# A one-core layer of recurrent attention and feed-forward: small matmuls placed between two weight chunks, a shorter GpSimd program, and one load cut in four

## The chip, the core and the metric

The kernel runs on one core of one Trainium2 chip. The metric is the device time of one execution in microseconds (us). Three runs of the kernel before gave 1005.17, 1005.47 and 1006.03 us; the median is 1005.47. Engines are named as in the profile: PE (TensorE) with PEld (its weight loads), DVE (VectorE), ACT (ScalarE), POOL (GpSimd), SP (the engine that only issues transfers here).

## The reference, cut to what matters

```python
def _A_ref(x, mem0, Wq, Wk, Wv, Wo, seg_len):      # 32 heads of 128, seg_len 32, 8 memory rows
    mem = mem0
    for s in range(n_seg):                          # 64 segments, one after another
        h = jnp.concatenate([mem, x[:, 32*s:32*s+32]], axis=1)      # 40 rows
        q, k, v = (einsum('btd,dhe->bhte', h, W) for W in (Wq, Wk, Wv))
        p = softmax(where(mask, q @ k^T * scale, -1e9))
        o = einsum('bhte,hed->btd', p @ v, Wo)
        mem = o[:, :8]                              # the next segment starts from it
        outs.append(o[:, 8:])
h  = x + _A_ref(layernorm(x), mem0, Wq, Wk, Wv, Wo, 32)
h2 = h + relu_glu(layernorm(h), W_gate, W_up, W_down)               # 640 -> 1728 -> 640
```

x has 2048 rows of 640 numbers, bf16. The 64 segments form one chain, since the 8 memory rows of one segment are inputs of the next.

## The kernel before

The whole program is written out by hand, with no loop left on the chip: `add` appends an operation to the list of one engine, `solve` finds which earlier operations it has to wait for, and each engine then runs its list in order. What follows on a list never passes what stands before it.

The kernel has three parts.

1. The opening. SP issues the three attention weights in chunks of 1 MB (five for each of K, Q and V, the chunks cutting the 640 rows into 128s), then eight pieces of the output weight Wo, then rows of x. `project` multiplies a set of 32 rows by one chunk for all heads; the K and Q products of three row sets follow the chunks as they land. `first_values` does the value products: chunks 0 to 2 in L770, chunks 3 and 4 in L896, behind the scores of segment 0 (`scores`, L894 and L895). Then come the softmax of segment 0, the products with the values (`pv_mem`), and the output product for the memory rows: `wo_pairs` in four groups (L920) into bank T0, and `wo_pass` for the other half of the heads into bank P3. Between these stand calls of `keep_busy`, whose products nobody reads: they are written to bank T1 over and over. With cut 2 each of its 512-column products is issued as two of 256 columns, with cut 4 as four of 128. `fold_split(T0, ...)` and `to_act_split(1, P3)` turn the result into the 8 memory rows of segment 1.

2. The segments 1 to 63, L945 on. Each segment projects its rows by K, Q and V, takes scores and softmax, and multiplies by Wo. The end of a segment is the narrow place: `wo_split` and `wo_pass` on PE; then DVE transposes a bank into TA (L602), ACT moves a part of it into SA (L604), SA is summed up (L606, on POOL in most segments and on DVE where s % 4 is 1), DVE transposes the other bank into TBf (L614) and adds SA to it (L615, the tile act_r). The next segment's first projection reads act_r. POOL's list in a segment is short: a wait, the copy `late_q` into Qo (L483), in some segments the copy `late_o` into oTe (L563), a wait, and the sum L606. In segment 60 (NSEG - 4) POOL also copies rows of act_r into act_e (L1087); segment 61 projects them.

3. The feed-forward, from segment 62 on mixed with the last segments. Its first block of 512 normalised rows was put aside in xn2_d and is loaded into xn2T by one transfer in segment 62 (L996); the gate and up weights are loaded in pieces from L1031 on. `gate_up` waits for all four keys of xn2T.

Before all this POOL writes the masks: `mca` by affine_selects (L298 and L302), then `mbd`.

The parts that the change and the prediction touch stand below.

Of the kernel before, what the change touches and what calls it, by code (L numbers as in the profile page):

```python
# [9 lines left out]
ALU = mybir.AluOpType  # L10
# [16 lines left out]
class _Graph:  # L27
# [10 lines left out]
    def add(self, eng, fn, r=(), w=(), dma=False):  # L38
        if eng == "pool" and not dma:
            r, w = tuple(r) + (("pool",),), tuple(w) + (("pool",),)  # L40
        op = _Op(eng, fn, tuple(r), tuple(w), dma)
        self.ops.append(op)
        return op
# [120 lines left out]
def build_kernel(nc, A_x, A_mem0, A_Wq, A_Wk, A_Wv, A_Wo, A_seg_len, B_W_gate, B_W_up, B_W_down, out):  # L164
# [3 lines left out]
    SEG = int(A_seg_len)  # L168
    F = B_W_gate.shape[1]
    assert (S, D, M, H, Dh, SEG, F) == (2048, 640, 8, 32, 128, 32, 1728)  # L170
    NSEG = S // SEG
    DC = D // 128
# [12 lines left out]
    xn2_d = nc.dram_tensor("xn2_d", [128, DC, TB], BF16)  # L185
# [9 lines left out]
    W = ar.alloc("W", [128, 3, DC, HD], BF16)  # L195
# [6 lines left out]
    xn2T = [ffn.alloc("xn2T0", [128, DC, TB], BF16)]  # L202
# [18 lines left out]
    mca = ar.alloc("mca", [128, 4, 2, SEG], BF16)  # L221
# [34 lines left out]
    def bank(b):  # L256
        return ps[:, b * 512:(b + 1) * 512]
# [5 lines left out]
    T0, T1 = 2, 3  # L263
    P0, P1, P2, P3 = 4, 5, 6, 7
# [8 lines left out]
    add = G.add  # L273

    def B(n):
        return ("B", n)
# [7 lines left out]
    for i in range(2):  # L284
        add("dve", lambda v, i=i: v.memset(oT[i][:], 0.0), w=[("oT", i, n, kh) for n in "mx" for kh in range(2)])
        add("pool", lambda p, i=i: p.memset(act_r[i][:], 0.0),
            w=[("act", i, j, "m") for j in range(4)] + [("act", i, "x")] + [("act", i, "x", j) for j in range(4)])
# [6 lines left out]
    for g in range(4):  # L294
        for j in range(4):
            for r in range(2):
                sl, n = mca[32 * g:32 * g + 32, j, r, :], 0 if r == g % 2 else 1 + j
                add("pool", lambda p, sl=sl, n=n: p.affine_select(sl, sl, [[1, SEG]], ALU.is_ge, 0.0,  # L298
                                                                  base=M if n == 0 else M * (n - 1) - RID,
                                                                  channel_multiplier=-1), r=[("mca",)], w=[("mca",)])  # L300
                if n > 1:
                    add("pool", lambda p, sl=sl, n=n: p.affine_select(sl, sl, [[0, SEG]], ALU.is_ge, 0.0,  # L302
                                                                      base=-M * (n - 1), channel_multiplier=1),
                        r=[("mca",)], w=[("mca",)])
    add("pool", lambda p: p.memset(mbd[:], 0.0), w=[("mbd",)])
    for g in range(4):
        for lo, hi, c in ((0, 1, g), (1, 5, g ^ 1)):
            add("pool", lambda p, g=g, lo=lo, hi=hi, c=c: p.memset(mbd[32 * g:32 * g + 32, lo:hi, 8 * c:8 * c + 8], BIG),
                r=[("mbd",)], w=[("mbd",)])
        for n in range(1, 5):  # L310
            sl = mbd[32 * g:32 * g + 32, n, :]
# [11 lines left out]
    def dma(dst, src, r=(), w=(), eng="sp"):  # L323
        add(eng, lambda e: e.dma_start(dst, src), r=r, w=w, dma=True)  # L324
# [121 lines left out]
    def place(s):  # L446
        return (s - 2) // 4 % 2, (s - 2) % 4
# [17 lines left out]
    def scores(s, hf, ks=range(4)):  # L465

        p, _ = place(s)

        def f(pe):
            for k in [4 * hf + n for n in ks]:  # L470
                for a in range(2):
                    for g in range(4):
                        h = head(k, g)
                        o, q = 160 * (g % 2) + 40 * (k % 4), 32 * (g ^ a)
                        i = pe.matmul(bank((P0, P1)[hf])[q:q + 32, o:o + 40],  # L475
                                      (Ko if a == 0 else Ke[p])[:, h, :], Qo[:, h, :], start=True, stop=True,
                                      skip_group_check=True)
            return i
        add("pe", f, r=[("Ko", hf), ("Qo", hf), ("Qo", "e"), ("Ke", p, hf)], w=[B((P0, P1)[hf])])
# [120 lines left out]
    def fold_split(bk, eng):  # L600

        add("dve", lambda v: v.transpose(TA[:].rearrange("p b c j -> p (b c j)"), bank(bk)[:, 0:320]), r=[B(bk)], w=[("TA",)])  # L602
        for lo, to in SWAP:
            add("act", lambda a, lo=lo, to=to: a.activation(SA[to:to + 64], TA[lo:lo + 64, 1, :, 0:M], ACTF.Copy),  # L604
                r=[("TA",)], w=[("SA", to)])
        add(eng, lambda v: v.tensor_tensor(SA[:], SA[:], TA[:, 0, :, 0:M], ALU.add), r=[("TA",), ("SA", 0), ("SA", 64)],  # L606
            w=[("SA", 0), ("SA", 64)])
        for lo, to in SWAP:
            add("act", lambda a, lo=lo, to=to: a.activation(fold[to:to + 64].rearrange(flat), bank(bk)[lo:lo + 64, 160:320],
                                                            ACTF.Copy), r=[B(bk)], w=[("fold",)])  # L610
# [138 lines left out]
    xe, xke = act_e[0], [("acte", 0)]  # L749
# [16 lines left out]
    def first_values(chunks):  # L766
        for c in chunks:
            for (a, ks), bks in zip((PASSES[0], PASSES[2]), OB[2]):
                project(a, ks, 2, (0, 1), bks, (c,))
# [109 lines left out]
        add("dve", lambda v: v.tensor_tensor(hT[par][:, j, :], g1[gi][:, :], bank(bu), ALU.mult),  # L879
            r=[B(bu), ("g1", gi)], w=[("hT", par, j)])  # L880

    def keep_busy(n, cut=1):
        wide = 512 // cut

        def f(pe):
            for g in range(4 * n):
                o = 32 * (g % 4)
                for q in range(cut):
                    i = pe.matmul(bank(T1)[o:o + 32, 0:wide], xe[:, 0, :], W[:, 2, 0, 0:wide], start=True, stop=True,  # L889
                                  skip_group_check=True)  # L890
            return i
        add("pe", f, r=xke + [("W", 2, 0)], w=[B(T1)])

    scores(0, 0)  # L894
    scores(0, 1)  # L895
    first_values(range(3, DC))  # L896
    for hf in range(2):
        exp_mem(0, hf)
        mask_mem(0, hf)
# [19 lines left out]
    for g in range(4):  # L919
        wo_pairs(0, T0, g)  # L920
        if g:
            keep_busy(4, (1, 2, 2, 4)[g])
    fold_split(T0, "pool")
    for g in range(3):
        wo_pass(0, P3, (1,), (g,))
# [19 lines left out]
    for s in range(1, NSEG):  # L945
# [16 lines left out]
        if s > 0:  # L962
            a, ks = pass_act(s)
            held, parts = fill_of(s)
            for i in range(2):
                project(a, ks, 1, (i,), ((P2, P3)[i],), *WAYS[i], held=i == 1 and held[0], parts=parts[i])
                to_tok((P2, P3)[i], i, "act")
                if last and i == 1:
                    load_piece(("Ko", 0), "act")
                flip(i, Ko, i, [("Ko", i)])  # L970
            if s % 4 == 2 and more:
                row_std(n_rows(nb + 1))
                row_scale(xl, ("xl",), n_rows(nb + 1), xl, ("xl",), "pool")
            if s % 4 == 1 and e2 is not None:
                row_std(128)
                row_scale(xt, ("xt",), 128, xt, ("xt",), "pool")
            pv_x(s - 1, 0)
            norm_x(0)
            if s % 4 == 0 and e2 is not None:
                add_attn(xt[:, :], xt, at, [("xt",), ("at",), ("rx",)], [("xt",)], "pool")  # L980
                dma(h_d[128 * e2:128 * e2 + 128, :], xt[:, :], r=[("xt",)], w=[("h_d", e2)])
            if s % 4 == 2:
                merge_v(s, 1)
            if not last:
                for i in range(2):
                    project(a, ks, 0, (i,), ((P0, P1)[i],), *WAYS[i], held=i == 1 and held[1], parts=parts[2 + i])
                    to_tok((P0, P1)[i], 2 + i, "act")
                    flip(2 + i, Qo, i, [("Qo", i)])
                    if i == 0:
                        norm_x_late(0)  # L990
                        flip_ox(s - 1, (0,))
            else:
                norm_x_late(0)
                flip_ox(s - 1, (0,))
            if s == NSEG - 2:
                dma(xn2T[0][:, :, :], xn2_d[:, :, :], r=[("xn2_d", u) for u in range(4)] + [("Wdone", 0)],  # L996
                    w=[("xn2", 0, u) for u in range(4)])
            project(a, ks, 2, (0,), (P2,), range(4), held=not last and held[2])
            scores(s, 0, (0, 1))
            project(a, ks, 2, (0,), (P2,), (4,))  # L1000
            scores(s, 0, (2, 3))
            if not last:
                exp_mem(s, 0)
                mask_mem(s, 0)
            to_v(P2, Vp, 0, ("Vp",), "act")
            if last:
                load_piece(("Vp", 0), "act")
            if s % 4 == 1 and ln:
                flip_rows(chunks_of(at[:, :]), xl, ("xl",), ("at",))
                if more:  # L1010
                    ln1_load(nb + 1, xl, ("xl",))
# [39 lines left out]
        if s == NSEG - 2:  # L1051
            p = 1 - place(s + 1)[0]
            add("pool", lambda o, p=p: o.tensor_copy(Qo[:, :, M:32], Qe[p][:, :, M:32]), r=[("Qe", p, i) for i in range(2)],
                w=[("Qo", i) for i in range(2)])
# [8 lines left out]
            dma(xt[:, :], x_ap[128 * e2:128 * e2 + 128, :], w=[("xt",)])  # L1063
            load_attn(at, e2, [], ("at",))
        wo_split(par, P1)
        fold_split(P1, "dve" if s % 4 == 1 else "pool")
        wo_pass(par, P3, (1,))
        to_act_split(s + 1, P3)
        if s >= 1:
# [15 lines left out]
        if s == NSEG - 4:  # L1085
            p, j = place(NSEG - 1)
            add("pool", lambda o, p=p, j=j: o.tensor_copy(act_e[1 - p][:, :, M:32], act_r[p][:, j, :, M:32]),  # L1087
                r=[("act", p, "x", j), ("act", p, "x")], w=[("acte", 1 - p)])


    def down_part(par, u, bks, js, hfs=(0, 1)):
# [71 lines left out]
    s = NSEG - 1  # L1163
# [37 lines left out]
    for b in range(NBLK):  # L1201
# [4 lines left out]
        for j in range(FC):  # L1206
# [8 lines left out]
            if b == 0 and j == 5:  # L1215
                for q, src in enumerate((B_W_gate, B_W_up)):
                    for e in range(2):
                        r0 = FR * (q ^ e)
                        dma(Wt[:, e, :, r0:r0 + FR], src[:, FM:F].rearrange("(c p) f -> p c f", p=128),
                            r=[("Wdone", 0), ("hT", 0, 5)], w=[("Wt", q, e)])  # L1220
# [74 lines left out]
```

## Time and profile before

One execution was profiled: 1004.47 us in all, of which the span from the first to the last instruction is 1002.7 us.

| what | value |
|---|---|
| span of the profiled execution | 1002.7 us |
| its time in all | 1004.47 us |
| runs shown (3) | 1005.17 to 1006.03 us, median 1005.47 |
| busy: DVE, ACT, POOL | 715.6, 524.9, 167.8 us |
| opening, up to the first K product of segment 1 | 0 to 58.33 us |
| attention segments, up to the first gate product | to 813.44 us |
| feed-forward | to the end |
| one segment, from its first product with values (L663) to the next | 12.03 to 12.33 us; 13.1 us for the one that ends at segment 63 |
| PE instructions: matmuls and weight loads | 26097 and 24920 |

A row of the timeline gives start, duration, engine, line, operation, tiles, shape and count; in brackets at its end stand the engine's idle time before it and what ended that. In the chain of waits each piece has a start, a duration and a name; "issue" means that nothing the profile shows was waited for. The row of a stretch gives its bounds, its length, the busy time of each engine with its count of instructions, the granted TensorE clock, the share of the DMA engines' time, and GB/s.

### The profile page before, as it was taken

The page shows a single profiled execution, that of the slowest core. Times are in us where ns is not written, and L with a number is a line of the kernel's source. Part 1 is how long each engine was busy: PE and PEld are TensorE (multiplying, and loading weights), DVE is VectorE, ACT ScalarE, POOL GpSimd, SP SyncE. Part 2 cuts the span into 40 slices and gives each one's busy share as a digit, 9 for nine tenths or more (in the row PEclk, how much of TensorE's full clock was granted, in tenths as well). Part 3 has the DMA queues.
Part 4 walks back from the last instruction along what each step waited for, and adds up shares of the span by engine and source line. Part 5 has one row for each costly group of instructions (what it writes and reads, how often), then busy time and mean ns, then how long its engine had stood idle before and what let it go on. Part 6 is the DMA issues. An engine that isn't in the chain of part 4 may idle for free.

```text
span 1002.7 us, 56369 instructions
## 1 busy us (share of the span) xinstructions
PE 970.9 (97%) x26097; PEld 537.8 (54%) x24920; DVE 715.6 (71%) x1863; ACT 524.9 (52%) x1330; POOL 167.8 (17%) x416
## 2 busy tenths in 40 slices
PE   3789999999999999999999999999999999999998
PEld 1255555556555555555556555655555554344443
DVE  2558787878888887888788878787878756345332
ACT  0456666666666666666666666566666643122121
POOL 7011202021302130222022212111110010000000
PEclk9899999999999999999999999999999999999999
DMA  9921212121222122111312131211121168413100
GB/s 374 417 96 36 53 29 53 28 56 55 54 41 54 48 54 46 48 54 47 53 41 63 48 55 40 41 41 39 40 40 34 44 175 242 103 20 93 27 14 26
DMA packets 73103, 73.34 MB, mean 73 GB/s; under 512 B 42304, under 2 KB 59680, under 8 KB 70944
## 3 DMA queue, kind: packets, MB, share of 16 engines
q1 hardware_dynamic: 70736, 68.44, 24.5%
q8 instruction: 200, 3.28, 1.4%
q10 hardware_dynamic: 2128, 1.31, 0.5%
q14 instruction: 39, 0.32, 0.1%
HBM read 37.04 MB, written 6.55 MB: 43 GB/s over the span
## 4 chain that ended last, share of the span: by engine, by line
PE 93%; DMA 3%; SPq 2%; DVE 1%; issue 1%; ACT 0%; POOL 0%; DVEq 0%; ACTq 0%
PE ps L386 47%; PE ps L850 10%; PE ps L359 7%; PE ps L574 7%; PE ps L591 7%; PE ps L634 4%; PE ps L1100 3%; DMA W<-in_A_Wv_dram 3%; PE ps L475 2%; PE ps L663 2%; PE ps L528 2%; SPq L324 1%; DMA Wd<-in_B_W_down_dram 0%; PE ps L889 0%; PE ps L863 0%
## 5 line engine op out<-in xcount | busy, mean ns | idle before, releaser
L386 PE MATMUL ps<-W,act_r 128*32 128x512 bf16 (+1 forms) x8369 | 454.4, 358 | 2.9 <-DVE act_r L615 1.8
L386 PEld LDWEIGHTS ps<-W,act_r 128*32 128x32 bf16 x8369 | 212.9, 96 | 168.3 <-DVE act_r L615 33.1
L410 ACT ACTIVATE tok<-ps 128x512 bf16<-128x512 f32 x190 | 109.4, 594 | 57.1 <-PE ps L386 48.7
L386 PE MATMUL ps<-W,act_e 128*32 128x512 bf16 x1224 | 120.8, 385 | 8.2 <-DMA W<-in_A_Wv_dram 4.2
L405 DVE STREAM_TRANSPOSE Ko<-tox 128x512 bf16<-128x512 bf16 x128 | 89.8, 702 | 38.9 <-ACT tox L410 36.6
L483 POOL COPY Qo<-Qe 128x256 bf16<-128x256 bf16 x64 | 28.0, 437 | 529.4 <-DVE oT L548 522.4
L410 ACT ACTIVATE tox<-ps 128x512 bf16<-128x512 f32 x134 | 79.6, 598 | 53.1 <-PE ps L386 32.0
L554 DVE STREAM_TRANSPOSE oT<-tox 128x512 bf16<-128x512 bf16 x128 | 94.2, 736 | 0.0
L405 DVE STREAM_TRANSPOSE Qo<-tok 128x512 bf16<-128x512 bf16 x124 | 85.5, 690 | 0.8
L359 PE MATMUL ps<-W,act_e 128*32 128x512 bf16 x856 | 85.5, 387 | 0.0
L574 PE MATMUL ps<-Wo,oT 128*32 128x160 bf16 x4032 | 82.4, 233 | 0.9 <-issue 0.9
L591 PE MATMUL ps<-Wo,oT 128*32 128x320 bf16 x2016 | 80.4, 300 | 0.0
L574 PEld LDWEIGHTS ps<-Wo,oT 128*32 128x32 bf16 x4032 | 71.4, 97 | 9.7 <-DVE oT L548 3.1
L410 ACT ACTIVATE Vp<-ps 128x512 bf16<-128x512 f32 x127 | 75.2, 592 | 0.7 <-ACT Vp L410 0.5
L878 ACT ACTIVATE g<-ps 128x512 bf16<-128x512 f32 x52 | 30.1, 593 | 80.1 <-PE ps L850 80.1
L604 ACT ACTIVATE SA<-TA 64x40 f32<-64x40 f32 x126 | 29.5, 234 | 75.8 <-DVE TA L602 75.0
L879 DVE TENSOR_TENSOR hT<-g,ps 128x512 bf16<-128x512 bf16 x52 | 35.7, 687 | 40.7 <-PE ps L850 38.7
L491 ACT ACTIVATE Pm<-ps 128x64 bf16<-128x64 f32 x126 | 28.2, 224 | 69.8 <-PE ps L475 69.7
L850 PE MATMUL ps<-xn2T,Wu 128*128 128x512 bf16 x259 | 64.5, 379 | 0.1
L850 PE MATMUL ps<-xn2T,Wg 128*128 128x512 bf16 x247 | 61.8, 379 | 1.3 <-issue 1.0
L591 PEld LDWEIGHTS ps<-Wo,oT 128*32 128x32 bf16 x2016 | 53.1, 97 | 15.3 <-DVE rm L538 0.9
L548 DVE STREAM_TRANSPOSE oT<-om 128x128 bf16<-128x128 bf16 x126 | 39.1, 310 | 31.1 <-ACT om L540 31.1
(113 smaller groups left out, 1441.0 us busy)
## 6 DMA issues: line engine op xcount, KB each, us to landing
VM<-Vp SPq DMA_DIRECT2D x126, 65.0 KB
VM<-Vp SPq DMA_DIRECT2D x63, 130.0 KB
W<-in_A_Wk_dram SPq DMA_DIRECT2D x5, 1024.0 KB
W<-in_A_Wq_dram SPq DMA_DIRECT2D x5, 1024.0 KB
W<-in_A_Wv_dram SPq DMA_DIRECT2D x5, 1024.0 KB
Wo<-in_A_Wo_dram SPq DMA_DIRECT2D x8, 640.0 KB
attn_d<-wtok SPq DMA_DIRECT2D x248, 7.5 KB
xt<-in_A_x_dram SPq DMA_DIRECT2D x16, 160.0 KB
```

The costliest lines, as they stand in the source:

```text
L359: return pe.add_instruction(mybir.InstMatmult(name=nc.get_next_instruction_name(), engine=mybir.EngineType.PE, ins=[pe.lower_ap(rhs), pe.l ...
L386: ins = pe.matmul(*b, start=(c == ends[0]), stop=(c == ends[1]), skip_group_check=True)
L405: add("dve", lambda v: v.transpose(dst[:, 16 * i:16 * i + 16, 0:32], tok[t][:, :].rearrange("p (h f) -> p h f", f=32)), r=tok_keys(t), w=keys)
L410: add("act", lambda a: a.activation(dst, src, ACTF.Copy), r=r, w=w)
L548: add("dve", lambda v: v.transpose(ap(oT[par], 160 * hf, [[40, 4], [320, 4], [1, 8]]), ap(om, 128 * hf, [[1, 4], [4, 32]])), r=[("om", hf) ...
L554: add("dve", lambda v, kh=kh: v.transpose(ap(oT[p], 160 * kh + M, [[320, 4], [40, 4], [1, 32]]), ap(tox, 128 * kh, [[256, 4], [1, 4], [4, ...
L574: i = pe.matmul(bank(bk)[32 * gg:32 * gg + 32, 0:160], src[:, hb, 0:32], w[:, gg], start=(hb == CH[16 * halves[0]]), stop=(hb == CH[-1]), ...
L591: i = pe.matmul(bank(bk)[32 * q:32 * q + 32, 0:320], src[:, hb, 0:32], w, start=(n == 0), stop=(n == 7), skip_group_check=True)
L634: ins = pe.matmul(bank(bk)[32 * q:32 * q + 32, 0:320], src[:, hb, 0:32], w[:, 2 * (q % 2):2 * (q % 2) + 2], start=(i == 0), stop=(i == 15) ...
L850: ins = pe.matmul(bank(bk), w[:, c, lo:lo + 128], xn2T[par][:, c, :], start=(c == 0), stop=(c == DC - 1))
L878: add("act", lambda a: a.activation(g1[gi][:, :], bank(bg), ACTF.Relu), r=[B(bg)], w=[("g1", gi)])
L879: add("dve", lambda v: v.tensor_tensor(hT[par][:, j, :], g1[gi][:, :], bank(bu), ALU.mult), r=[B(bu), ("g1", gi)], w=[("hT", par, j)])
```

## The change

Five edits:

- `keep_busy` loses its cut and gets a number of columns. The calls between the groups of `wo_pairs` issue 16 products of 512 columns each (before: 32 of 256, 32 of 256, 64 of 128). A new call of 80 products of 32 columns stands between value chunk 3 and value chunk 4. PE's list has as many instructions as before.
- In `mca`, four affine_selects of 32 columns become one over 4 x 32. POOL's list is three instructions shorter from there on.
- The load of xn2T in segment 62 becomes four transfers: chunks 0, 1, 2, and 3 with 4.
- L606 of segment 61 goes from DVE to POOL.
- The copy L1087 also waits for segment 61's memory rows in act_r (L615).

```diff
+                pat = [[1, SEG]]
+                if g == 0 and n == 0:
+                    if j:
+                        continue
+                    sl, pat = mca[0:32, :, r, :], [[0, 4], [1, SEG]]
-                add("pool", lambda p, sl=sl, n=n: p.affine_select(sl, sl, [[1, SEG]], ALU.is_ge, 0.0,
+                add("pool", lambda p, sl=sl, n=n, pat=pat: p.affine_select(sl, sl, pat, ALU.is_ge, 0.0,
...
-    def keep_busy(n, cut=1):
-        wide = 512 // cut
+    def keep_busy(n, cols=512):
...
             for g in range(4 * n):
                 o = 32 * (g % 4)
-                for q in range(cut):
-                    i = pe.matmul(bank(T1)[o:o + 32, 0:wide], xe[:, 0, :], W[:, 2, 0, 0:wide], start=True, stop=True,
-                                  skip_group_check=True)
+                i = pe.matmul(bank(T1)[o:o + 32, 0:cols], xe[:, 0, :], W[:, 2, 0, 0:cols], start=True, stop=True,
+                              skip_group_check=True)
...
-    first_values(range(3, DC))
+    first_values((3,))
+    keep_busy(20, 32)
+    first_values((4,))
...
         wo_pairs(0, T0, g)
         if g:
-            keep_busy(4, (1, 2, 2, 4)[g])
+            keep_busy(4)
...
             if s == NSEG - 2:
-                dma(xn2T[0][:, :, :], xn2_d[:, :, :], r=[("xn2_d", u) for u in range(4)] + [("Wdone", 0)],
-                    w=[("xn2", 0, u) for u in range(4)])
+                for n, (lo, hi) in enumerate(((0, 1), (1, 2), (2, 3), (3, DC))):
+                    dma(xn2T[0][:, lo:hi, :], xn2_d[:, lo:hi, :], r=[("xn2_d", u) for u in range(4)] + [("Wdone", 0)],
+                        w=[("xn2", 0, n)])
...
-        fold_split(P1, "dve" if s % 4 == 1 else "pool")
+        fold_split(P1, "dve" if s % 4 == 1 and s != NSEG - 3 else "pool")
...
-                r=[("act", p, "x", j), ("act", p, "x")], w=[("acte", 1 - p)])
+                r=[("act", p, "x", j), ("act", p, "x"), ("act", *place(s + 1), "m")], w=[("acte", 1 - p)])
```

## The prediction, made before the changed kernel ran

> **What bounds the kernel.** I began with the page's busy times, its chain and its queues:
>
> ```profile
> PE 970.9 (97%) x26097; PEld 537.8 (54%) x24920; DVE 715.6 (71%) x1863; ACT 524.9 (52%) x1330; POOL 167.8 (17%) x416
> ...
> q8 instruction: 200, 3.28, 1.4%
> ...
> PE 93%; DMA 3%; SPq 2%; DVE 1%; issue 1%; ACT 0%; POOL 0%; DVEq 0%; ACTq 0%
> ```
>
> PE sets the time, so what counts is where PE stands still or runs at a lower clock. The second row is the program itself: 3.28 MB in 200 packets is 16 KB each, and 26097 + 24920 = 51017 PE instructions over 200 packets are 255 each, so q8 brings PE's code in pages of about 256 instructions. Next the chain of waits, in the opening and around segment 62:
>
> ```profile
> 14.26 28.38 DMA W<-in_A_Wv_dram
> 42.64 0.04 issue
> ...
> 51.98 1.50 issue
> ...
> 805.21 0.92 issue
> ```
>
> The opening waits for value chunk 4 until 42.64. The two long "issue" pieces are stops of PE in the middle of a row of like products, with no semaphore to wait for. Beside them I put the trace's records of q8's packets and PE's list counted out (a product with its own weight load is two). Counted so, the stops lie a whole number of 256s apart (186 of them); they are page borders, those of pages 4 and 190. A packet starts at 51.02 and takes 1.10, and PE resumes at 53.47; another starts at 803.76, takes 0.89, and PE resumes at 806.13. So a page can be used about 1.35 to 1.5 us after its packet ends. A page's packet follows the moment at which PE enters the page before it: usually 0.4 to 1.4 us later, but 3.5 us later (37.96 to 41.49, 47.49 to 51.02) while the weights stream, and 2.0 us (801.77 to 803.76) behind the xn2T load.
>
> Third, POOL around three ends of segments:
>
> ```profile
> 178.45 0.27 POOL L606 TENSOR_TENSOR SA<-SA,TA 128x40 f32<-128x40 f32 x1 [0.47 <-ACT SA L604]
> ...
> 190.78 0.27 POOL L606 TENSOR_TENSOR SA<-SA,TA 128x40 f32<-128x40 f32 x1 [0.76 <-DVE TBf L614]
> ...
> 202.82 0.27 POOL L606 TENSOR_TENSOR SA<-SA,TA 128x40 f32<-128x40 f32 x1 [0.46 <-ACT SA L604]
> ```
>
> The middle one comes 0.29 us late (idle 0.76 against 0.47), with its input ready; it is on the chain (190.79, 0.27, POOL SA L606), and the segment takes 12.33 instead of 12.04. The same is seen at 384.02 and 577.18, each 128 POOL instructions later, which is the size of an 8 KB page of the other engines (q14).
>
> Fourth, the clock and PE's work in stretches of 3.41 us:
>
> ```profile
> 35.53:38.95 3.42, 1.98 (x82) 0.71 (x62) 0.86 (x2) 0.00 (x0) 0.00 (x0) 1.00 1.01 422
> 38.95:42.36 3.41, 1.36 (x52) 0.41 (x33) 0.63 (x4) 1.00 (x4) 0.00 (x0) 1.00 1.00 410
> 42.36:45.77 3.41, 2.30 (x33) 0.71 (x28) 1.71 (x3) 1.20 (x2) 0.00 (x0) 0.50 1.02 411
> 45.77:49.19 3.42, 3.42 (x54) 1.70 (x41) 2.82 (x9) 2.37 (x3) 0.44 (x1) 0.50 1.02 416
> 49.19:52.60 3.41, 2.79 (x111) 2.52 (x104) 0.58 (x2) 2.79 (x6) 0.02 (x1) 1.00 1.01 409
> ```
>
> After a stretch with 1.36 us of PE work the granted clock is 0.50 for two stretches; after one filled with work it is 1.00 again.
>
> **The change, part by part.**
>
> *POOL's three instructions.* The three affine_selects themselves (0.20 to 0.27 each) end long before the masks are read and are worth nothing. But the page borders now fall three instructions later in the list: not at L606 but at the next segment's late_q copy (L483). That copy is read some 7 us later; 0.29 of delay to it, and to the late_o copy behind it, still lets L606 start in time (the copy at 189.63 would end at 190.32, and SA comes at 190.35). Gain 3 x 0.29 = 0.86. Bounds: 0 if the cost moves with L606, 0.9.
>
> *Segment 60's copy and segment 61's sum.* L615 at 782.44 takes 0.29 beside the copy L1087 at 782.40; at 794.66, with no copy beside it, 0.20. With the added wait the copy follows L615: 0.09. Behind the copy on POOL stand late_q and nothing due before 791; act_e is read by segment 61's fillers from 790 on. The sum on POOL is 0.27 against 0.20 on DVE, but no longer delays L614 there (794.16, 0.20, then 794.28); the fillers end at about the same time. Between 0 and 0.1; I take 0.05. Together 0.14, so that these and POOL make **1.0**.
>
> *Four transfers.* SP issues 4 instead of 1; the one took 0.58, neighbours 0.42 and 0.59, so 1.0 to 1.8 more. SP idles from 800.63 to 801.50 and from 801.92 to 803.27 (2.2 us), which hides it; the piece of Wg behind it slips by up to 1 us and is first read at 813.44. With that cover gone, the VM transfers at 803.27 would be late for 810.3. What it buys: in the records, xn2T's 128 packets of 5120 B run from 801.2 to 803.5 and the page asked for at 801.77 starts only when they are done. In pieces of 1 KB a share of one DMA engine is a fifth as long, and the page can go in between. At the usual 0.4 to 1.4 us it would start at 802.2 to 803.2 and be usable by 804.5 to 805.6; PE needs it at 805.21. Gain 0.5 to 0.92, and 0 if it goes behind all four anyway. I take **0.85**. The stall hides nothing else: the memory rows wait for L574 behind it.
>
> *The opening.* Removed: 80 matmuls with 80 weight loads; the columns are the same (2048 per group of 32 rows and call, 0.87 us in the chain at 50.18). Added: 80 products of 32 columns. The row nearest to these, L475 with 40 columns, has 64 in 0.46 us (38.59 to 39.05), so about 0.6 us, inside the wait from 41.26 to 42.64. By itself it is free. But 160 more instructions stand before chunk 4, and page 3, which before began in the first wo_pairs (47.49), now begins at the 49th of the 80 products, at about 41.5. Its packet should be where it was, 41.49 + 1.10, usable at 43.9 to 44.1. So PE stops inside the new call, does the rest (0.3 us), and begins chunk 4 at 44.3 instead of 42.69: **1.6 later**. In return page 4 is asked for at 44.0 instead of 47.49 and is there by 50.1, well before its border, now in the last wo_pairs at about 52: the stop of 1.50 goes. The clock: the watched stretch 38.95 to 42.36 has 1.36 + 0.4 of work instead of 1.36, and 1.98 was enough in the stretch before; nearer the former by little. I take it that the clock still drops, and returns at 49.19. Then: chunk 4 to the first pv_mem takes 2.67 (42.69 to 45.36), pv_mem 0.63, the first xe projection 1.71: 44.3 + 5.0 = 49.3. From there at full clock wo_pairs 0.53, then three times (0.87 + 0.27) less one 0.27 after the last: 0.53 + 2 x 1.14 + 0.87 = 3.7, ending at 53.0. Before, the last keep_busy ended at 53.95. So 0.95 is gained. A little is given back: page 5 came at 54.82 + 1.04, behind the last weights, usable at 57.3, and its border lies in the filler after the last wo_pass; the first K product of segment 1, at 58.33 before, can hardly start before 57.6. Gain of the opening **0.7**. Its bounds: a loss of 2.4 and a gain of 2.1 (rivals).
>
> Here one rule is weighed. The Trainium skill, "Runtime: NRT & Kernel Launch", section "Instruction fetch mechanics", has code come in 16 KiB blocks of 256 instructions and calls the cost of crossing a block border mostly hidden. The 1.50 us at 51.98 speak against it here. By that rule no stop arises in the new call either; what this would give is rival 2.
>
> *Sum.* 1.0 + 0.85 + 0.7 = 2.55. On the profiled execution's own time: span 1002.7 and 1.8 around it, 1004.47 - 2.55 = 1001.9. The median of the runs is 1.00 above the profiled one, so 1005.47 - 2.55 = **1002.9**.
>
> **Rivals.**
>
> 1. *The clock stays up.* The added work suffices and the clock does not drop at 42.36. Then from 44.3: chunk 4 and the copies 1.8, pv_mem 0.3, xe 0.87, wo_pairs and fillers 3.7, a last border met at 50.1: about 51.3, and page 5 holds segment 1 back to about 56.2: 2.1 instead of 0.7. Time 1001.5. For it: 1.98 sufficed. Against it: 1.36 + 0.4 is less.
> 2. *No stop in the new call*, because page 3 is there. Chunk 4 begins at 42.69, and from 47.70 on the chain runs without the 1.50 and its aftermath: 1.07 + 1.14 + 0.27 + 0.87 + 0.27 + 0.87 = 4.5, ending at 52.2, a gain of 1.75. Time 1001.8. Against it is the packet at 41.49.
> 3. *The clock stays down longer.* Chunk 4's delay leaves the stretch 45.77 to 49.19 with 2.4 us of work instead of 3.42 (the one before it had 2.30 and did not bring the clock back). If the clock returns at 52.60, the last filler ends at 54.65, a loss of 0.7: time 1004.3. If it returns only at 56.0, at 56.3, a loss of 2.4, which outweighs the 1.85 of the rest: **1006.0, slower**. That decides from a return at about 54.5 on. Against it: the stretch from 49.19 would be full.
> 4. *The change does not do what it says*: the page still waits behind all four transfers, or POOL's border still costs. Then 0.85 less: 1003.7.
>
> For the clock, "TensorE: Matmul & The Clock Gate" in the Trainium skill (Part 1) gives windows of 3413 ns that run free of the program, half clock after an idle window and full clock after a busy one. The two dim stretches (6.83 us) agree with the length, but a window with 1.36 us of work was no idle one, and it dropped all the same. By the rule's wording rival 1 would hold.
>
> **Chances and range.** Forecast 0.38; rival 1 0.15; rival 2 0.13; rival 3 0.18 to 1004.3 and 0.05 to the slower end; rival 4 0.11. The likeliest is 1002.9. The range goes from 1001.0 (rival 1 with half a microsecond for the spread of the runs) to 1005.0 (rival 3's nearer end with the same). A measurement of this kernel tells 0.2%, or 2.0 us, from no change; faster means below 1003.46. The forecast falls there with some four fifths of its weight, rivals 1 and 2 wholly: 0.30 + 0.28 = 0.58. Slower by over 2.0 us needs more than rival 3's far end: 0.06. The rest, 0.36, is within 0.2%.
>
> **What would show it.** Right: an issue stop of about 2.4 us inside the 80 small products near 41.5, none at 52, chunk 4's products from about 44.3; half clock from 42.36 to 49.19; L606 near 190.8, 384 and 577 with 0.47 of idle, and no segment of 12.33; no stop among the L574 products near 805. Wrong: small products that run through and chunk 4 at 42.7; a clock that returns elsewhere; a stop at another border; or a segment 62 still 0.9 longer, with the page behind the four loads.

## The result, and the profile after

| | before | after |
|---|---|---|
| median of the runs (13 each) | 1005.29 us | 1002.92 us (1001.44 to 1005.6) |
| ratio of the runs | | 0.9979, 95% interval 0.997 to 0.9989 |
| profiled execution, its span | 1004.47, 1002.7 us | 1002.29, 1000.4 us |
| first K product of segment 1 | 58.33 | 57.65 |
| first gate product | 813.44 | 811.24 |

One run of before took 1433.78 us, far from all its others, and the ratio leaves it out.

On a second chip the same two kernels gave 1004.64 and 1002.00 us (run e9_after below; ratio 0.9977, interval 0.9966 to 0.9987). By these ratios the change is worth 2.1 and 2.3 us of 1005. Both intervals lie below 1, but the gain is of the size that the prediction called the least a measurement of this kernel can tell (2.0 us).

By the two profiled executions 0.68 us were gained up to the first K product of segment 1, 1.52 from there to the first gate product (811.24 - 57.65 = 753.59, against 755.11), and 0.16 behind it. In the code of after, lines from the masks on stand five lines further down (L606 is now L611, L574 is L579); the small products are L892.

The page of after, the rows that answer to the first of before:

```profile
PE 971.2 (97%) x26111; PEld 535.9 (54%) x24920; DVE 715.4 (72%) x1862; ACT 524.4 (52%) x1330; POOL 167.5 (17%) x414
...
q8 instruction: 200, 3.28, 1.4%
...
PE 93%; DMA 3%; SPq 1%; DVE 1%; issue 1%; ACT 0%; DVEq 0%; ACTq 0%
```

Work and code are the same: 200 pages still, and PE is as busy as before. All that changed lies in the gaps. The chain of waits of after (start, duration, what):

```profile
12.25 28.68 DMA W<-in_A_Wv_dram
40.98 0.40 PE ps L391 x4
...
42.02 0.35 PE ps L892 x48
42.37 2.45 issue
44.82 0.38 PE ps L892 x32
45.20 0.25 PE ps L391 x4
...
802.27 1.09 PE ps L596 x32
803.36 1.15 PE ps L579 x64
```

The opening's stop has moved: instead of 1.50 us at 51.98 there are 2.45 us at 42.37, after exactly 48 of the 80 small products, and chunk 4 (the L391 at 45.20 here; the timeline has its start at 45.02) waits behind them. In the chain of after the 64 products of L579 run in one piece at 803.36, where before had a stop of 0.92 us among them near 805.

POOL around the same three ends of segments as before, from the timeline (start, duration, engine, line, operation, tiles, shape, count, idle before it and what ended it):

```profile
177.75 0.27 POOL L611 TENSOR_TENSOR SA<-SA,TA 128x40 f32<-128x40 f32 x1 [0.47 <-ACT SA L609]
...
189.86 0.27 POOL L611 TENSOR_TENSOR SA<-SA,TA 128x40 f32<-128x40 f32 x1 [0.47 <-ACT SA L609]
...
201.92 0.27 POOL L611 TENSOR_TENSOR SA<-SA,TA 128x40 f32<-128x40 f32 x1 [0.47 <-ACT SA L609]
```

The middle sum is no longer 0.29 us late. The three segments that took 12.33, 12.32 and 12.33 us take 12.11, 12.04 and 12.04.

The clock in stretches of 3.41 us (columns as before: PE, PEld, DVE, ACT, POOL, granted clock, DMA share, GB/s):

```profile
36.09:39.50 3.41, 1.96 (x55) 0.56 (x40) 0.57 (x1) 0.00 (x0) 0.00 (x0) 1.00 1.01 423
39.50:42.92 3.42, 1.94 (x132) 1.17 (x109) 0.63 (x4) 1.00 (x4) 0.00 (x0) 1.00 1.01 411
42.92:46.33 3.41, 1.27 (x48) 0.47 (x39) 0.63 (x2) 0.63 (x2) 0.00 (x0) 1.00 1.02 413
46.33:49.75 3.42, 2.82 (x44) 1.36 (x40) 2.84 (x10) 1.82 (x4) 0.44 (x1) 0.50 1.02 412
49.75:53.16 3.41, 3.41 (x84) 2.03 (x76) 1.55 (x4) 3.34 (x4) 0.00 (x0) 1.00 1.01 410
```

The stretch with the small products has 1.94 us of PE work and the clock stays; the next one holds the stop, has 1.27, and the clock drops, for one stretch instead of two.

### The profile page after: what moved, and what is told of

The parts are those of the page before. It is cut to its first block, busy times and chain, and to the rows that moved or that the text cites. A ratio compares the mean times of both kernels' runs of the same rounds, so it can differ in the third digit from the quotient of the medians.

```text
span 1000.4 us, 56384 instructions
## 1 busy us (share of the span) xinstructions
PE 971.2 (97%) x26111; PEld 535.9 (54%) x24920; DVE 715.4 (72%) x1862; ACT 524.4 (52%) x1330; POOL 167.5 (17%) x414
## 4 chain that ended last, share of the span: by engine, by line
PE 93%; DMA 3%; SPq 1%; DVE 1%; issue 1%; ACT 0%; DVEq 0%; ACTq 0%
PE ps L391 47%; PE ps L855 11%; PE ps L364 7%; PE ps L579 7%; PE ps L596 7%; PE ps L639 4%; PE ps L1106 3%; DMA W<-in_A_Wv_dram 3%; PE ps L480 2%; PE ps L668 2%; PE ps L533 2%; SPq L329 1%; DMA Wd<-in_B_W_down_dram 0%; PE ps L892 0%; PE ps L868 0%
## 5 line engine op out<-in xcount | busy, mean ns | idle before, releaser
L391 PE MATMUL ps<-W,act_r 128*32 128x512 bf16 (+1 forms) x8369 | 454.3, 358 | 2.0 <-DVE act_r L620 1.3
L391 PEld LDWEIGHTS ps<-W,act_r 128*32 128x32 bf16 x8369 | 212.8, 96 | 167.0 <-DVE act_r L620 32.5
L391 PE MATMUL ps<-W,act_e 128*32 128x512 bf16 x1224 | 120.2, 385 | 7.3 <-DMA W<-in_A_Wv_dram 3.7
L579 PE MATMUL ps<-Wo,oT 128*32 128x160 bf16 x4032 | 81.4, 233 | 0.0
L579 PEld LDWEIGHTS ps<-Wo,oT 128*32 128x32 bf16 x4032 | 70.6, 97 | 9.5 <-DVE oT L553 3.1
L855 PE MATMUL ps<-xn2T,Wg 128*128 128x512 bf16 x260 | 64.7, 379 | 0.0
```

The costliest lines, as they stand in the source:

```text
L391: ins = pe.matmul(*b, start=(c == ends[0]), stop=(c == ends[1]), skip_group_check=True)
L579: i = pe.matmul(bank(bk)[32 * gg:32 * gg + 32, 0:160], src[:, hb, 0:32], w[:, gg], start=(hb == CH[16 * halves[0]]), stop=(hb == CH[-1]), ...
L855: ins = pe.matmul(bank(bk), w[:, c, lo:lo + 128], xn2T[par][:, c, :], start=(c == 0), stop=(c == DC - 1))
```

## The experiments

Twelve experiments in three groups (the last four repeat kernels of the others with more runs, side by side); each group shared a chip and its runs of before. A part of the change is first added to before alone (e1 to e4), then taken out of after again (e7, e8, e11, e12), and the new call is put elsewhere (e5, e6, e10).

### One part alone

e1_pool3 is before with the merged affine_select, e2_four with the four transfers, e3_open with the opening's edit, e4_seg60 with the two edits of segments 60 and 61. The diffs are the parts of the one shown above.

> The kernel before with the merged affine_select alone. Border theory: the page borders of POOL's list leave the sum L606, which starts 0.13 us after its ACT input near 191, 384 and 577 (before: 0.42 to 0.43), no segment takes 12.3 us, and the time falls by 0.86 us. Rival, the work itself: 0.8 us less of POOL work in the opening changes nothing on the chain, the late sums stay or move to another segment's sum, and the time stays within 0.2 us.

> The kernel before with the four transfers alone. Page theory: the packet of PE's page asked for at about 801.8 starts within 1.4 us instead of 2.0, the stop among the L574 products of segment 62 shrinks from 0.92 to at most 0.4 us, and the time falls by 0.5 to 0.9 us. Rival, the page waits for all transfers: the stop stays at 0.9 us and the time does not move.

> The kernel before with the opening's edit alone (80 small products between the value chunks, no cut products). Forecast: a stop of 2.4 us after 48 of the 80 small products, none in the later fillers, the first K product of segment 1 about 0.7 us earlier (17.4 instead of 18.1 us after value chunk 3 begins); the time falls by 0.7 us in the profile, by 0 to 1.5 in the median of runs, depending on for how many stretches of 3.41 us the clock is halved. Rival, that most of the measured gain is here: 1.4 us or more.

> The kernel before with the two small edits of segments 60 and 61. Forecast: L615 of segment 60 takes 0.20 us instead of 0.29, the segment lengths that were 12.16 and 12.12 become 12.06 and 12.05, the late sums on POOL and the stop near 805 stay. Rival: the edits move nothing, the lengths stay at 12.16 and 12.12.

| | median (runs) | ratio to before, 95% | first K product | half clock in the opening |
|---|---|---|---|---|
| e1_pool3 | 1003.83 (12) | 0.9992 [0.9981, 1.0003] | 58.87 | 52.20 to 55.61 |
| e2_four | 1003.81 (12) | 0.9991 [0.9981, 1.0001] | 57.64 | none |
| e3_open | 1003.67 (12) | 0.9989 [0.9979, 0.9999] | 57.11 | 37.97 to 41.38 |
| e4_seg60 | 1002.34 (1) | one run alone | 57.41 | 37.51 to 40.92 |

Before gave 1004.84 us there. By their ratios the three timed parts come to 0.8 + 0.9 + 1.1 = 2.8 us, against 2.1 and 2.3 for the whole change in its two measurements. Each of these numbers has an interval of about 1 us to both sides, so the sums agree within them, but two of the three parts alone can't be told from nothing, and the third barely. The profiles say more. In e1 the middle L611 is on time, while in e2, e3 and e4 it is late by 0.29 to 0.30 (idle 0.76 to 0.77), as in before. The line of e1:

```profile
190.98 0.27 POOL L611 TENSOR_TENSOR SA<-SA,TA 128x40 f32<-128x40 f32 x1 [0.47 <-ACT SA L609]
```

e3 has the new stop, again after 48 small products, of 1.79 us where 2.4 were expected. PE came to the border at about the same time as in after (42.26 and 42.37), but the page's packet ran earlier, from 41.47 to 42.55 against 42.30 to 43.33. The first K product stands 1.22 us before that of before's profile, and by time 1.1 us were gained; 0.7 were forecast, and the rival asked for 1.4 or more.

```profile
41.74 0.52 PE L887 MATMUL ps<-W,act_e 128*32 128x32 bf16 x48
44.05 0.38 PE L887 MATMUL ps<-W,act_e 128*32 128x32 bf16 x32 [1.79 <-issue]
```

e4's periods of the segments it touches went from 12.16 and 12.12 us to 12.06 and 12.03. One thing was a miss: in e2 the stop near 805 should have shrunk to at most 0.4 us, and 0.52 are left.

```profile
805.29 1.15 PE L574 MATMUL ps<-Wo,oT 128*32 128x160 bf16 x56 [0.52 <-issue]
```

The first three pieces are 384 packets of 1 KB, the fourth is 128 packets of 2 KB. In the records of the packets e2's page was asked for at 801.42, and its packet started at 802.75, behind 375 of the 384 and 19 of the 128. SP had begun to issue the four pieces 1.72 us before the request; in the seven other profiles with four pieces it was 1.06 to 1.58 us, and there the page's packet started 0.20 to 0.91 us after the request instead of 1.33. So the cut alone does not let the page pass, and how much it helps seems to hang on how early the request comes among the pieces. The two groups below show how often that is.

A second thing the four profiles show is the spread of the old opening. With the code of before, the stop at the old border (1.50 us in the profile of before) was 2.36 us in e1, 2.43 in e2 and 2.34 in e4: where the clock had not dropped between chunk 4 and the border, PE came to the border sooner and waited longer for the same page. The half-clock stretch lay elsewhere in each execution, and in e2 there was none.

### The new call elsewhere

e5_behind and e6_warm are after with

```diff
-    keep_busy(20, 32)
     first_values((4,))
+    keep_busy(20, 32)                  # e5
```
```diff
-    keep_busy(20, 32)
+    keep_busy(5)                       # e6
     first_values((4,))
+    keep_busy(15, 32)
```

> The changed kernel with the 80 small products placed behind value chunk 4 instead of before it; as many PE instructions up to every later point. Theory (a page border is what stops the new call: page 3's border lies at its 48th product, and the page is usable at about 44): PE meets that border only behind chunk 4's products, which then start as soon as the chunk is there, near 42.6 to 42.9 (45.02 in the changed kernel); the stop in front of chunk 4 is gone, what is left of it stands behind chunk 4 and is under 0.5 us; no stop of over 1 us near 52, since the added instructions still lie ahead of that border. First K product of segment 1 at 56.3 to 57.2 instead of 57.65, time 0.5 to 1.3 us below the changed kernel, if the half-clock stretch is no longer than 3.4 us. Rival (the stop at the 48th product comes from the wait for chunk 4 and the other work of that moment, not from the code page): chunk 4 starts as late as in the changed kernel, 44.3 or later, and the time is the same within 0.3.

> The changed kernel with the 80 small products split: 20 with 512 columns each (about 1.1 us of PE work by the 0.87 us that 16 take) before value chunk 4, 60 with 32 columns behind it. Same count of instructions. Theory (page border, and the clock set by the work of a 3.41 us stretch): the page border is met behind chunk 4, so no stop of over 0.5 us before it; the wait for chunk 4 holds 1.1 us more work, so that a stretch that had 1.27 to 1.36 now has over 2.3 and the clock does not drop there. Chunk 4 at 42.7 to 43.1, first K product of segment 1 at 55.8 to 57.0, time 1.0 to 2.0 us below the changed kernel. Rival (the small products' place matters, their work does not): half clock as often as in the version with all 80 behind chunk 4, and a time within 0.3 of that one. Second rival (20 wide products run at half clock and delay chunk 4): chunk 4 later than 43.5.

Both took away the stop in front of chunk 4, which then began at 42.92 and 42.94, when it was there. The stop of e6 is the cleanest sight of the border (from the timeline):

```profile
43.81 0.27 PE L892 MATMUL ps<-W,act_e 128*32 128x32 bf16 x16
44.32 0.49 PE L892 MATMUL ps<-W,act_e 128*32 128x32 bf16 x44 [0.24 <-issue]
```

From the start of the new call it comes after 20 wide products with their weight loads (40 instructions), chunk 4's 16 products with 8 loads (24) and 16 small ones (32): 96, as many as the 48 small products with their loads in after. The stop belongs to a place in the list, not to what is computed there.

The times: 1001.34 us (8 runs) and 1001.49 (10) against 1004.16, ratios 0.9971 [0.9961, 0.9981] and 0.9971 [0.9961, 0.9982]. Better than after (0.9979) by some 0.8 us by the point estimates, but the intervals overlap. The expected 0.5 to 1.3 and 1.0 to 2.0 us are not in the profiles either: the first K product stands at 57.50 and 57.20, against 57.65. In e6 the clock never dropped in the opening, and in e5's it was halved from 38.06 to 41.48; yet the two take the same time. So e6's first rival was right about the time, and work for the clock was worth nothing there that these runs can tell. To see where the removed stop went, after and e5's code were then run side by side.

### After, the call behind, and the parts taken back, on one chip

e9_after is the changed kernel itself, e10_behind the code of e5, e11_poolback (and e7_poolback, run once) after with POOL's list as long as before, e12_oneload (and e8_oneload, run once) after with the single load of xn2T.

```diff
-    add("pool", lambda p: p.memset(mca[:], BIG), w=[("mca",)])
+    for _ in range(4):                                            # e7, e11
+        add("pool", lambda p: p.memset(mca[:], BIG), w=[("mca",)])
```
```diff
-                for n, (lo, hi) in enumerate(((0, 1), (1, 2), (2, 3), (3, DC))):
-                    dma(xn2T[0][:, lo:hi, :], xn2_d[:, lo:hi, :], r=[("xn2_d", u) for u in range(4)] + [("Wdone", 0)],
-                        w=[("xn2", 0, n)])
+                dma(xn2T[0][:, :, :], xn2_d[:, :, :], r=[("xn2_d", u) for u in range(4)] + [("Wdone", 0)],     # e8, e12
+                    w=[("xn2", 0, u) for u in range(4)])
```

> The changed kernel with three memsets of the first mask tile added to POOL's list, which is then as long as before. Theory (128-instruction borders of POOL's code): the sum L611 of the segments that end near 190, 383 and 576 again shows an idle of 0.76 instead of 0.47, and the segments around them take 12.33 instead of 12.04, while all else in the opening and near 805 stays as in the changed kernel: span longer by 0.6 to 0.9. Rival (what went was the affine_selects' own work, or the late sums were chance): idle 0.47 at those three places and no period of 12.3.

> The changed kernel with xn2T again loaded by one transfer. Theory (the code page waits behind the 5120-byte packets of that load): the page asked for near 800.2 starts its packet about 2 us later (0.9 in the changed kernel) and PE stops 0.4 to 0.9 us in the middle of the like products near 803; the periods of the segment around it are longer by that. Rival (the stop near 805 went because the earlier shifts move the border into a wait): no stop near 803 to 805, the packet again within 1 us of the request, span as in the changed kernel within 0.3.

> The changed kernel itself once more, as the measure for the three beside it on the same chip. By the sum on record it lies 2.55 us below the kernel before (ratio 0.9975); by the runs so far 2.4 us (0.9979). Stop of 2.0 to 2.6 us after the 48th small product if the clock is full until then, shorter if a half-clock stretch lies ahead of it.

> The changed kernel with the 80 small products behind value chunk 4, timed beside the changed kernel on one chip. Theory (the stop at the code page is a loss of the new call's place): 0.5 to 1.0 us below the changed kernel. Rival (what the stop costs is hidden, since the opening then ends on the pieces of Wo that still come in: waits for them of 0.20, 0.48 and 0.45 us were seen): within 0.3 us of the changed kernel.

> The changed kernel with three memsets that make POOL's list as long as before, timed. Theory: three periods of 12.3 us (the ones that end at segments 12, 28 and 44), and 0.85 us above the changed kernel on the same chip (0.5 to 1.2). Rival (the segments take the 0.29 back later): the late sums are there but the time is within 0.3 of the changed kernel.

> The changed kernel with xn2T again loaded by one transfer, timed. Theory: a stop of 0.5 to 1.0 us near 803 to 805 and 0.5 to 0.9 us above the changed kernel on the same chip. Rival (the stop's time is got back where the feed-forward begins): the stop is there, and the time within 0.3 of the changed kernel.

| | median (runs) | median against e9 | ratio to before (1004.64), 95% |
|---|---|---|---|
| e9_after | 1002.00 (12) | | 0.9977 [0.9966, 0.9987] |
| e10_behind | 1001.87 (9) | -0.13 | 0.9972 [0.996, 0.9983] |
| e11_poolback | 1002.68 (12) | +0.68 | 0.9986 [0.9975, 0.9996] |
| e12_oneload | 1002.50 (12) | +0.50 | 0.998 [0.9971, 0.999] |

The ratios give other distances to e9: -0.5, +0.9 and +0.3 us. None of the three is clear of noise by time alone, so what follows rests on the profiles.

*Why the stop costs so little.* Rows of the timeline of e9, the changed kernel:

```profile
44.06 0.38 PE L892 MATMUL ps<-W,act_e 128*32 128x32 bf16 x32 [2.15 <-issue]
...
55.60 0.46 PE L579 MATMUL ps<-Wo,oT 128*32 128x160 bf16 x16 [0.37 <-DMA Wo<-in_A_Wo_dram]
55.89 1.03 PE L892 MATMUL ps<-W,act_e 128*32 128x512 bf16 x12
57.25 0.61 PE L391 MATMUL ps<-W,act_r 128*32 128x512 bf16 x10 [0.33 <-DVE act_r L620]
```

and of e10, with the call behind chunk 4:

```profile
42.95 0.40 PE L391 MATMUL ps<-W,act_e 128*32 128x512 bf16 x4 [1.44 <-DMA W<-in_A_Wv_dram]
...
43.82 1.00 PE L892 MATMUL ps<-W,act_e 128*32 128x32 bf16 x80
...
50.32 0.38 PE L892 MATMUL ps<-W,act_e 128*32 128x512 bf16 x1 [0.96 <-issue]
...
55.58 0.46 PE L579 MATMUL ps<-Wo,oT 128*32 128x160 bf16 x16 [0.47 <-DMA Wo<-in_A_Wo_dram]
...
57.22 0.61 PE L391 MATMUL ps<-W,act_r 128*32 128x512 bf16 x10 [0.36 <-DVE act_r L620]
```

e10 begins chunk 4 at 42.95 instead of 44.27, gives 0.96 us back at the next border, and then both kernels wait for the same thing: the last piece of Wo, until 55.60 and 55.58. The first K product follows at 57.25 and 57.22. In this pair the rival of e10 holds: the stop is hidden behind the weights that still come in at 410 GB/s. It is not hidden everywhere. In after, e7 and e12, where half clock lasted to 49.75 or longer, PE waits for no piece of Wo at the end, and the first K product stands at 57.59 to 57.77. And the runs leave room for a small gain: the three measurements with the call behind chunk 4 (e5, e6, e10) have ratios of 0.9971 to 0.9972 and no run above 1003.17 us, the two of after 0.9979 and 0.9977 with runs up to 1005.6. Whether the call behind is better by some 0.5 us thus stays open.

The trace's records of the code packets show a second chain just as long. From entering a page to being able to use the next one takes some 6 us while the weights stream (3.6 for the packet to start, 1.0 to 1.1 for the packet, 1.2 to 1.5 until PE goes on): e10 enters pages 3, 4 and 5 at 44.34, 50.32 and 56.46. 256 matmuls and weight loads stand between the last two. So PE could not have been at the end of the opening much earlier even without the wait for Wo. That fewer instructions would shorten that chain, and finer pieces of Wo the other, was not tried.

This floor also says what the opening's edit seems to have done. In the seven profiles with it as in after (after, e3, e7, e8, e9, e11, e12) the first K product stands at 57.11 to 57.77, mean 57.47, wherever the half clock fell, in e7 and e12 for two whole stretches (43.38 to 50.2 and 43.1 to 49.9). In the four without it (before, e1, e2, e4) it stands at 57.41 to 58.87, mean 58.06. Those with no late half-clock stretch (e2: 57.64, e4: 57.41) are as good as after. By these eleven executions the edit does not move the best case but takes away the bad ones, in which a late half-clock stretch came on top of a stop at page 4's border (before and e1). The likely reason is that an early entry into page 3 asks for page 4 early; two bad executions are too few to call it shown.

*POOL.* e11 has the three late sums again (this is the one near 190; in e7 it stands at 190.20 with 0.75), and periods of 12.34, 12.33 and 12.32:

```profile
190.08 0.27 POOL L612 TENSOR_TENSOR SA<-SA,TA 128x40 f32<-128x40 f32 x1 [0.76 <-DVE TBf L620]
```

All 14 profiles agree. The six whose list on POOL is as long as in before (before, e2, e3, e4, e7, e11) have just these three late sums, of 0.75 to 0.77, and three segments of 12.3 us there; the eight with the shorter list have none. (Single segments of 12.24 to 12.32 us at other places stand in e2, e7, e8 and e9, without a late sum; what lengthened those is not known.) The 0.68 us of e11 against e9 lie in the expected 0.5 to 1.2; the intervals of the two overlap. e7's one execution was 1.8 us longer than after's in its span, where 0.6 to 0.9 were expected; besides the 0.79 of the three segments it waits 1.60 us for Wd at 850.44 where after's waits 0.45 at 848.66, so that only the first part is POOL's.

*The load.* e12 has the stop back in its old place, longer than the expected 0.5 to 1.0, and so has e8 (0.97 us up to 804.38, expected 0.4 to 0.9):

```profile
803.30 0.32 PE L579 MATMUL ps<-Wo,oT 128*32 128x160 bf16 x8
804.96 1.15 PE L579 MATMUL ps<-Wo,oT 128*32 128x160 bf16 x56 [1.34 <-issue]
```

All six profiles with the single load have this stop, of 0.58 to 1.34 us (mean 0.87); of the eight with four loads only e2 has one. From request to packet the page took, in the six profiles with the single load, 1.99 (before), 1.61 (e1), 1.64 (e3), 1.60 (e4), 2.07 (e8) and 2.41 us (e12); with four loads 0.91 (after), 0.89 (e9), 0.85 (e5), 0.75 (e11), 0.55 (e6), 0.26 (e7) and 0.20 (e10), and 1.33 only in e2, which alone of these has the old opening and the old segments 60 and 61. The single load's 128 packets were all ahead of the page in before and e12, and 81 to 105 of them in the others. With four, 5 to 250 of the 384 small ones were, and none of the 128 larger, but for e2. The time between e12 and e9 is 0.50 us by the medians, the lower edge of what was expected, and 0.3 by the ratios; the intervals overlap here too.

## Why the prediction came out right, and where it did not

*POOL: right in mechanism and size.* 0.86 forecast; 0.22 + 0.28 + 0.29 = 0.79 in the profiles of before and after, 0.68 by the medians of e11 and e9. The border, now at another instruction, costs nothing there. Segments 60 and 61: 0.14 forecast, and 0.12 + 0.09 = 0.21 in the two periods.

*Four transfers: right mechanism, size a little high in this profile.* The page came 0.91 us after its request, inside the forecast 0.4 to 1.4, and was used at 803.36 without a stop. But the packet of the page after it started 2.12 us behind its own request, at 805.48, and took 1.40 us, and about there PE stood still once more:

```profile
808.19 0.65 PE L668 MATMUL ps<-VM,Px 64*32 64x129 bf16 x32 [0.43 <-DVE Ko L410]
```

The profile puts this wait down to the DVE's Ko, which ended at 808.07; but in e9 the same L668 began at 807.62, while the like Ko ran from 807.27 to 807.98, so it does not need Ko. A page usable 1.3 us after its packet's end at 806.88 would fit; that this was the cause is not shown. The period up to segment 63 went from 13.13 to 12.67, by 0.46 of the forecast 0.85; in e9 it was 12.20, by 0.93. The term's lower bound, "0 if it goes behind all four anyway", was nearly met once, in e2: 0.52 of stop were left, where e3 and e4, with the single load, had 0.64 and 0.58.

*The opening: right sum, wrong way, so that the size was in part luck.* The stop "of about 2.4 us" came with 2.45, at the 49th product as counted; the stop at 52 went; chunk 4 began 4.04 us after chunk 3 (45.02 and 40.98) instead of 2.48 (42.69 and 40.21): 1.56, forecast 1.6. And the gain was 0.68 where 0.7 was forecast. What failed is the step between, "I take it that the clock still drops, and returns at 49.19". Over the 14 profiles, each cut on its own grid of 3.41 us from 27 us on, the opening's stretches at full clock with at most 1.48 us of PE work (1.05 to 1.48, twelve of them) were all followed by half clock, and those with 1.55 or more by none. The two nearest to the edge, from e8 and e7, each with the stretch behind it:

```profile
41.51:44.93 3.42, 1.48 (x100) 1.00 (x88) 0.00 (x0) 0.00 (x0) 0.00 (x0) 1.00 1.02 410
44.93:48.34 3.41, 2.63 (x41) 0.67 (x24) 2.60 (x7) 1.21 (x3) 0.00 (x0) 0.50 1.04 418
...
36.55:39.96 3.41, 1.55 (x80) 0.87 (x72) 0.68 (x4) 0.56 (x3) 0.00 (x0) 1.00 1.01 420
39.96:43.37 3.41, 1.40 (x64) 0.75 (x57) 0.34 (x3) 0.44 (x2) 0.00 (x0) 1.00 1.02 412
```

The forecast's 1.36 + 0.4 = 1.76 should have been read as enough: rival 1's condition. Even from the two stretches known then, 1.76 lies nearer to the 1.98 that sufficed than to the 1.36 that did not; "nearer the former" was a slip. The clock dropped all the same, one stretch later, since the stop itself emptied that one (1.27); that no rival had. And the grid lay elsewhere: in after its borders stand 0.56 us later against the program than in before. With half clock for one stretch rather than two, 1.45 us were gained from chunk 3 to the first K product (16.67 against 18.12), twice the forecast; chunk 3 itself came 0.77 later from the DMA, and the two together made the 0.68. The mean over the profiles, 58.06 - 57.47 = 0.59, says that 0.7 was about right for the kernel, but not for the reason given; and with four and seven executions this mean is itself rough.

*The rivals.* 1 and 2 were priced past the floor. Rival 1 held segment 1 back to "about 56.2" by page 5 alone, and rival 2 had 1.75 us of gain. Where neither the clock dropped nor a stop stood before chunk 4 (e6, e10) the first K product came at 57.20 and 57.22, 1.1 us before that of before's profile: the last piece of Wo sets that, and the prediction did not have it. Rival 3 may have come true in single runs: two of the 13 of after with a mean clock of 0.995 (an estimated 10 us at half speed, 0.005 x 1003 / 0.5) took 1004.05 and 1005.6 us, near its 1004.3 and 1006.0. But no trace shows where these 10 us lay, and a third run took 1005.52 us at a clock of 0.997. Rival 4 was e2's case, by a part.

The Trainium skill, "Runtime: NRT & Kernel Launch", section "Instruction fetch mechanics", calls the cost of crossing into a new block of code mostly hidden. The 2.45 us at 42.37 in after and the 1.34 up to 804.96 in e12 disagree: the first stands where weights stream at 410 GB/s, the second behind the 640 KB of xn2T. Elsewhere it agrees: the first is the only "issue" stop of over 0.1 us in after's 200 pages, though the 0.43 us at 808.19 may be another under a different name.

"TensorE: Matmul & The Clock Gate" in the Trainium skill (Part 1) has an idle window bring half clock, on a grid that runs free of the program. The free grid agrees: half clock began at 42.36, 46.34, 52.20, 37.97 and 37.51 in five executions of nearly one opening. The idle window does not: 1.48 us of work in 3.41 dropped the clock.

## What to carry to other kernels

Count instructions as well as time: where code pages come behind a full DMA queue, moving instructions without adding any moves the stops, and PE can be predicted to stop at a known instruction. Before pricing a stop, ask for the next thing that ends the stage (here the last weight piece), since what lies ahead of it is worth no more than the distance to it. And where a clock grid runs free of the program, one profile is one draw: compare the step over several executions before reading its size.

## What had not been expected of the hardware

- In the opening of these 14 profiles, stretches of 3.41 us at full clock with up to 1.48 us of PE work were followed by half clock, and those with 1.55 us or more were not. At half clock, stretches with 2.14 and 2.30 us of work were followed by another half, and those with 2.63 us or more by full clock.
- A page of PE's code took about 6 us from request to use while weights streamed at 410 GB/s, and 4.7 us behind the single load of xn2T (800.25 to 804.96 in e12), though it is one packet of 16 KB that itself took 1.0 to 1.1 us in the first case and 0.92 in the second.
- Four loads instead of one let that packet start after 5 to 250 of their 512 packets in seven of eight profiles (394 in e2); one load of larger packets kept it back until 81 to 128 of its 128 had started.
